# Spectrum channels grouped by parity, the second half's first inverse stage on 64-row tiles, and a new instruction order behind the first MLP

## The chip, the cores and the metric

The kernel runs on one core of a Trainium2 chip. The core has five instruction streams: TensorE (PE, matmuls, with its weight loads listed apart as PEld), ScalarE (ACT), VectorE (DVE), GpSimd (POOL) and SyncE (SP, which here only issues DMAs). The on-chip memory SBUF has 128 partitions; PSUM, where matmuls write, has 8 banks of 512 fp32 per partition. The metric is device microseconds of one execution, the median over several runs.

## The reference

The input `x` is 2048 tokens by 512 channels, bf16. Two kinds of layer alternate twice, each on a layer-normed copy and with a residual:

```python
x = A_q
x = x + _A_ref(_layernorm(x), A_k, A_v, A_shift_k, A_ssm_k, A_ssm_D)
x = x + _B_ref(_layernorm(x), B_w1, B_b1, B_w2, B_b2)
x = x + _A_ref(_layernorm(x), ...)      # the same weights again
x = x + _B_ref(_layernorm(x), ...)
...
# _A_ref: a 4-tap shift of k times v, a causal convolution over all 2048 tokens by FFT, times q
kv = k_shift * v
y = irfft(rfft(kv_pad) * rfft(ssm_k_pad))[:2048]
return q * (y + kv * ssm_D)
# _B_ref: gelu(layernorm(x) @ w1 + b1) @ w2 + b2, 512 -> 1376 -> 512
```

The convolution's `y` depends on `k`, `v` and the filters alone, so it is computed once and used by both A layers.

## The kernel before

**The convolution.** The tokens are cut into two halves of 1024, and the FFT into two stages of small DFTs, all as matmuls. For the filter (tags `h1`, `h2`) and for `kv` (`x1`, `x2`) `stage1` (line 553) makes DFTs over 128 tokens for eight sub-sequences, `stage2` (line 565) combines the eight with the table S2. Channels go in 64 groups of 8. After `stage2` a partition stands for a triple: one of 8 frequencies, one of the 8 channels `d` of a group, and real or imaginary part (the lowest bit). DVE multiplies the two spectra (line 464, 2048 elements wide), and for the second half adds a second product (tag `sum`). The inverse goes in two stages again: `inverse1` (line 665) with the table U, `inverse2` (line 683) with the table T2. `inverse1` is called once per half (tags `i1_0` and `i1_1`). One call makes 8 PSUM tiles of two banks; a tile is 8 groups of channels times two terms (cosine and sine side), that is 16 matmuls whose weights are the spectrum, 128 by 128 and read in steps of 4 elements (8 bytes), and whose moving operand is 128 columns of U. Each tile is evicted by one instruction of 1024 elements (line 469 on ACT, line 470 on DVE). In U a column of channel `d` has nonzero entries only in rows of the same `d`.

**Small filters.** The 4-tap shift is done on PE too. `shift` (line 610, first half) sends 11 shifted copies to each of two 64-row tiles of the array; per row tile the 11 moving operands have 2048 columns together, so 22 matmuls and 4096 columns a call. `shift_pair` (line 638, second half, tags `fir4` to `fir7`, two calls) uses four 32-row tiles: 88 matmuls and 8192 columns a call. Its keys come by eight transposing DMAs (line 766, tag `kt`), its values by plain loads on the same queue, and DVE multiplies its result with the values (line 647). `stage1` uses two column tiles (128 rows by 64 columns), all other matmuls the whole array.

**The MLPs.** Tokens go in 13 blocks: first half (1, 1, 2, 2, 2) row tiles of 128 tokens in layer pair one and (2, 2, 2, 2) in pair two, second half (4, 4) and (4, 4). For block b the tags are `q`b (statistics and norm), `y`b (times y, residual), `z`b (second norm), then `m1` (line 886: 11 tiles of 4 matmuls, N = 128 times the block's row tiles, Gelu on ACT, line 891) and `m2` (lines 920 and 909: 11 matmuls of 512 columns per row tile, issued in pieces of 4, 4 and 3, then an add on DVE, line 924). The normed rows are transposed by DMA (line 866), the first two by PE (line 874). The first-half blocks use nothing from `i1_1`; they fill PE while the second half's convolution is made. Block 9 is the first to read the second half's `y`, which comes from `inverse2` tagged `i2_1`.

**The order.** Every operation is numbered in program order. A constant list `SEQ` gives the order in which the 1185 operations go to their engines' in-order queues; a string `ENGS` chooses ACT, DVE or POOL where there is a choice; a string `BANKS` gives each PSUM tile its first bank. Waits follow from these: an operation waits for what it reads, and for the eviction of the tile that had its banks before. Numbers that matter below: `fir5` 296 and `fir7` 303 (the two `shift_pair` matmul groups), `x1_1` 308 to 322 (even: PE, odd: eviction), `x2_1` 324 to 355 with the sums 327, 331, ... 355, `i1_1` 356 to 371 (even: PE, odd: eviction, all eight on ACT), `i2_1` 372 to 381.

In the order of before, PE's eight `i1_1` tiles stand in two runs, one tile and then seven, with one piece of `m2` between. Their banks (each tile takes two) are 6, 4, 6, 2, 4, 6, 2, 4. Blocks that use split arrays behind the first MLP, each between whole-array work: [fir5], [one `x1_1` tile, then fir7], [one `x1_1`], [three], [three].

Of the kernel before, what the change touches and what calls it, by code (L numbers as in the profile page):

```python
# [36 lines left out]
class Prog:  # L37
# [60 lines left out]
    ENGS = ("apvpvvvpavaavaaaaaavvvaaavvvpvpvaavaaaaavaavvaaaaaaaavavaaaaaavaaavaaaaaappppaaaaaaaaaaaaaaaaaaaaaaaaaaaaapvvp"  # L98
            "paappvppaappvvvpaappaappaappaappaappaappvavpaappvappaappvvppvvvpaappvvavvvvvvavpvvvvppavavpvvvvvpvaaavpvvaaapv"
            "avva")  # L100
    BANKS = ("02220326464004602026041320002442462264542202240064064646402046462667062260046446220462640604660406064226644472"
             "44450442172316353547502206314500451400554567076567013226140174645320543403764701436154766316307007062272260403"
# [243 lines left out]
def _tables():  # L346
# [10 lines left out]
    S2 = np.zeros((2, 8, 8, 128, 2, 8, 8))  # L357
# [603 lines left out]
```

## Time and profile before

| | |
|---|---|
| median of 3 runs | 239.22 us (239.12 to 239.52) |
| span of the profiled execution, first to last instruction | 238.6 us |
| PE busy | 226.9 us |
| PE weight loads busy (beside PE) | 152.3 us |
| DVE busy | 178.1 us |
| ACT busy | 159.6 us |
| POOL busy | 55.3 us |
| matmuls of `inverse1`, both halves | 15.0 us, 256 |

The profile comes from one execution; what the runs show beyond its span (239.22 - 238.6 = 0.6 us) lies before the first and behind the last instruction. Its views used here: the page (shares, and the span in 40 slices whose digits are tenths of busy time), the chain of work that ended last (start, length and line of each piece), the groups by line and shape (xcount, then busy us and mean ns of one), timelines of one engine, and windows (busy time of each engine in a stretch). Matmul durations are latencies of pipelined instructions, so a rate is read from the length of a piece of the chain divided by its count. A few matmul records are missing, so a piece's count can be one short (x87 for 88).

### The profile page before, as it was taken

How to read it: one execution, taken by the hardware profiler on the slowest of the kernel's cores; microseconds unless marked ns; L12 is line 12 of the kernel's file. 1: busy time of each engine (PE TensorE's matmuls, PEld its weight loads, DVE VectorE, ACT ScalarE, POOL GpSimd, SP SyncE). 2: the span in 40 equal slices, each digit the busy share in tenths (PEclk: the TensorE clock that was granted, in tenths of full speed). 3: DMA queues.
4: the chain of work that ended last, by engine and by line, in shares of the span. 5: the costliest groups of instructions: out<-in, count | busy, mean ns of one | idle time of the engine just before them, and what ended most of it. 6: DMA issues, size and time to landing. Idle time of an engine off the chain costs nothing.

```text
span 238.6 us, 6251 instructions
## 1 busy us (share of the span) xinstructions
PE 226.9 (95%) x2615; PEld 152.3 (64%) x2637; DVE 178.1 (75%) x358; ACT 159.6 (67%) x255; POOL 55.3 (23%) x120
## 2 busy tenths in 40 slices
PE   6998698899999999999999999999999999999995
PEld 3897588885968588667769675644445444444454
DVE  0579869999999999999999999593579469404013
ACT  2586879999996899999768786359036606831630
POOL 2421030104623506446004522303020210200000
PEclk9999979999999999999999999999999999999999
DMA  6999767989946660053100304200300050132202
GB/s 173 350 393 388 272 181 186 257 267 194 163 87 197 153 140 3 1 69 103 54 0 15 80 0 83 49 3 12 78 0 3 18 157 0 25 66 91 84 0 91
DMA packets 41112, 26.75 MB, mean 112 GB/s; under 512 B 23702, under 2 KB 33788, under 8 KB 41084
## 3 DMA queue, kind: packets, MB, share of 16 engines
q1 hardware_dynamic: 40786, 26.20, 40.5%
q8 instruction: 21, 0.34, 0.6%
q10 hardware_dynamic: 298, 0.16, 0.3%
q14 instruction: 7, 0.06, 0.1%
HBM read 15.07 MB, written 2.10 MB: 72 GB/s over the span
## 4 chain that ended last, share of the span: by engine, by line
PE 83%; DVE 6%; DMA 4%; ACT 3%; issue 2%; POOL 1%; SPq 1%; POOLq 0%
PE ps L886 32%; PE ps L920 31%; PE ps L665 6%; PE ps L553 5%; PE ps L565 3%; ACT ar L469 3%; DMA ar<-in_A_ssm_k_dram 2%; DVE ar L464 2%; DMA ar<-ar 2%; DVE ar L616 1%; PE ps L683 1%; PE ps L909 1%; PE ps L638 1%; PE ps L610 1%; DVE ar L470 1%
## 5 line engine op out<-in xcount | busy, mean ns | idle before, releaser
L891 ACT ACTIVATE ar<-ps,sm 128x256 bf16<-128x256 f32 (+4 forms) x143 | 65.4, 525 | 41.0 <-PE ps L886 39.5
L469 ACT ACTIVATE ar<-ps 128x1024 bf16<-128x1024 f32 (+3 forms) x77 | 71.3, 1005 | 16.4 <-PE ps L553 6.4
L886 PE MATMUL ps<-ar 128*128 128x256 bf16 (+4 forms) x568 | 81.5, 297 | 0.3
L920 PE MATMUL ps<-ar 128*128 128x512 bf16 (+1 forms) x324 | 77.2, 379 | 1.1 <-issue 0.3
L886 PEld LDWEIGHTS ps<-ar 128*128 128x128 bf16 (+1 forms) x572 | 52.8, 100 | 28.1 <-ACT ar L891 0.4
L464 DVE TENSOR_TENSOR ar<-ar 128x512 bf16<-128x512 bf16 (+3 forms) x105 | 62.7, 637 | 0.9 <-ACT ar L469 0.4
L920 PEld LDWEIGHTS ps<-ar 128*128 128x128 bf16 (+1 forms) x341 | 32.4, 98 | 33.4 <-ACT ar L891 0.2
L924 DVE TENSOR_TENSOR ar<-ar,ps 128x512 bf16<-128x512 bf16 x31 | 20.7, 678 | 33.2 <-PE ps L920 33.0
L797 DVE BATCH_NORM_STATS2 sm<-ar 128x6 f32<-128x512 bf16 x64 | 42.9, 683 | 0.5
L822 ACT ACTIVATE ar<-ar,sm 128x512 bf16<-128x512 bf16 x34 | 26.4, 811 | 9.5 <-DVE sm L809 8.3
L804 POOL TENSOR_TENSOR sm<-sm 128x2 f32<-128x2 f32 (+2 forms) x26 | 23.6, 909 | 23.8 <-DVE sm L802 22.0
L802 POOL TENSOR_SCALAR sm<-sm 128x2 f32<-128x2 f32 (+2 forms) x21 | 6.4, 304 | 97.3 <-DVE sm L798 97.1
L553 PE MATMUL ps<-ar 128*64 128x128 bf16 x512 | 18.6, 227 | 3.1 <-issue 1.4
L565 PEld LDWEIGHTS ps<-ar 128*128 128x128 bf16 x512 | 18.4, 102 | 3.4 <-ACT ar L469 1.0
L565 PE MATMUL ps<-ar 128*128 128x64 bf16 x512 | 19.6, 199 | 0.5 <-ACT ar L469 0.4
L553 PEld LDWEIGHTS ps<-ar 128*64 128x64 bf16 x512 | 15.7, 114 | 6.1 <-issue 2.6
L812 POOL TENSOR_SCALAR sm<-sm 128x1 f32<-128x1 f32 x43 | 16.1, 390 | 2.0
L470 DVE CAST ar<-ps 128x1024 bf16<-128x1024 f32 x11 | 13.3, 1222 | 4.3 <-PE ps L565 2.8
L665 PE MATMUL ps<-ar 128*128 128x128 bf16 x256 | 15.0, 219 | 0.5 <-DVE ar L464 0.4
L665 PEld LDWEIGHTS ps<-ar 128*128 128x128 bf16 x256 | 14.7, 113 | 1.2 <-DVE ar L464 0.6
L823 DVE TENSOR_SCALAR ar<-ar,sm 128x512 bf16<-128x512 bf16 x30 | 11.8, 410 | 3.4 <-POOL sm L812 3.1
L470 DVE COPY ar<-ps 128x1024 bf16<-128x1024 bf16 (+1 forms) x9 | 5.5, 632 | 8.0 <-PE ps L516 5.3
(41 smaller groups left out, 94.3 us busy)
## 6 DMA issues: line engine op xcount, KB each, us to landing
ar<-tab_s SPq DMA_DIRECT2D x16, 256.0 KB, 9.0
ar<-ar SPq DMA_DIRECT2D x16, 256.0 KB, 3.7
ar<-in_A_ssm_k_dram SPq DMA_DIRECT2D x8, 256.0 KB, 6.8
ar<-in_A_q_dram SPq DMA_DIRECT2D x8, 256.0 KB, 4.7
ar<-in_A_v_dram SPq DMA_DIRECT2D x8, 256.0 KB, 6.1
out_dram<-ar SPq DMA_DIRECT2D x7, 256.0 KB, 2.5
ar<-in_B_w_dram SPq DMA_DIRECT2D x4, 344.0 KB, 4.8
ar<-in_B_w_dram SPq DMA_DIRECT2D x5, 256.0 KB, 4.0
```

What stands on the lines that cost most here:

```text
L464: return P.op(eng, lambda e: e.tensor_tensor(o, a, b, op), dur, reads=[a, b] + list(more), writes=[o])
L469: return e.activation(dst, src(), AF.Copy)
L470: return e.tensor_copy(dst, src())
L553: r = e.matmul(Q(tl, 64 * ri, 64, i * 128, [1, 128]), w, m, start=True, stop=True)
L565: r = e.matmul(Q(tl, 0, 128, i // 8 * 512 + i % 8 * 4, [32, 16], [1, 4]), w, m, start=True, stop=True)
L665: r = e.matmul(Q(tl, 0, 128, i * 128, [1, 128]), w, m, start=n == 0, stop=n == 1)
L797: P.op(DVE, lambda e, sj=sj, x=x: e.bn_stats(sj, x), 600.0, reads=[x], writes=[sj])
L804: P.op(POOL, lambda e: e.tensor_tensor(r, v, hf, ALU.pow), 420.0 + 149.0 * n, reads=[v, hf], writes=[r])
L822: return e.activation(o, x, AF.Identity, bias=u, scale=r)
L886: r = e.matmul(Q(tl, 0, rows, 0, [1, w]), a, m, start=dk == 0, stop=dk == 3)
L891: P.op(ACT, lambda e, dst=dst, tl=tl, rows=rows, bias=bias, w=w: e.activation(dst, Q(tl, 0, rows, 0, [1, w]), AF.Gelu_apprx_tanh, bias=bia ...
L920: r = e.matmul(Q(tl, 0, 128, 0, [1, 512]), ins[fc][0], ins[fc][1], start=fc == 0, stop=fc == 10)
```

## The change

Three things change.

1. **Tables.** In S2's output order and U's row order the partition index becomes (channel d, frequency, real/imaginary) in place of (frequency, d, real/imaginary), with the channels of a group in the order 0, 2, 4, 6, 1, 3, 5, 7. So all even channels of a group stand on partitions 0 to 63 and all odd ones on 64 to 127. The tables keep their sizes; real and imaginary part remain neighbours, as the swapping DMAs of the spectrum need.
2. **`inverse1` for the second half** (`split=True`). Each 128-row matmul with 128 columns becomes two 64-row ones with 64 columns: rows 0 to 63 with the columns of even channels, rows 64 to 127 with those of odd channels. The columns are picked from U in steps of 2 elements, and the two results go to the tile's two banks. A tile has 32 matmuls. Its eviction reads PSUM in runs of 32 and writes SBUF in steps of 2 elements (4 bytes).
3. **The order.** `SEQ` is as before in its first 330 places, up to the first MLP, and different behind; `ENGS` and `BANKS` differ in the same part. In the new order PE's `i1_1` tiles stand in two runs of four, the banks being 2, 4, 6, 2 and 4, 2, 6, 4: `368, 366, 364, 360`, then the last pieces of `m2` for two row tiles (682, 686), then `370, 358, 356, 362`, then three pieces of `m2` (735, 736, 737), then `i2_1` with 380. ACT evicts them in the order 369, 367, 361, 365, 371, 359, 357, 363. Split-array blocks behind the first MLP: [fir5], [one `x1_1` tile, then fir7], [four `x1_1`], [three], [four `i1_1`], [four `i1_1`]. `fir5` stands earlier among the MLP's matmuls, and the eight `kt` transposes stand earlier on SP's queue. The first MLP's `m1` tiles (N = 128) stand 19 in a row on PE, 17 before. The last `m2` piece of one row tile (686) stands ahead of `i1_1` before and between its two runs after, and two `y7` operations of DVE move from ahead of the last sum to behind it.

```diff
     SEQ = (
...
-        404, 450, 406, 489, 422, 451, 295, 532, 405, 423, 466, 407, 586, 460, 408, 454, 414, 467, 456, 294, 490, 491, 446,
...
-        345, 629, 660, 349, 661, 658, 754, 342, 355, 384, 327, 751, 382, 335, 719, 350, 346, 752, 755, 351, 347, 343, 331,
-        753, 721, 756, 715, 757, 758, 720, 759, 716, 727, 725, 632, 728, 383, 677, 664, 633, 665, 674, 801, 760, 726, 662,
-        733, 799, 672, 856, 659, 761, 663, 675, 668, 669, 666, 729, 680, 670, 860, 673, 762, 734, 763, 671, 667, 684, 678,
-        766, 800, 723, 802, 764, 730, 717, 731, 857, 858, 679, 685, 724, 862, 803, 718, 861, 859, 713, 714, 681, 686, 366,
-        722, 682, 732, 368, 863, 804, 367, 805, 864, 865, 866, 364, 806, 369, 360, 767, 809, 365, 810, 361, 358, 359, 765,
-        356, 357, 362, 370, 807, 811, 735, 808, 363, 812, 371, 683, 867, 813, 736, 374, 372, 737, 373, 873, 376, 868, 738,
...
+        451, 295, 282, 290, 289, 286, 207, 291, 283, 292, 285, 287, 586, 405, 416, 294, 293, 423, 448, 417, 456, 412,
...
+        727, 718, 680, 730, 355, 751, 713, 723, 675, 351, 667, 715, 714, 719, 728, 347, 725, 724, 721, 720, 733, 726,
+        343, 684, 734, 716, 731, 331, 685, 732, 722, 755, 681, 633, 752, 368, 753, 366, 369, 756, 860, 364, 367, 799,
+        360, 757, 682, 361, 801, 686, 365, 800, 759, 370, 758, 760, 358, 683, 371, 761, 762, 356, 802, 858, 359, 362,
+        803, 856, 763, 735, 357, 766, 804, 861, 857, 767, 859, 736, 764, 363, 862, 805, 737, 806, 765, 809, 863, 807,
+        380, 864, 810, 865, 811, 376, 381, 808, 814, 372, 377, 866, 739, 812, 876, 813, 873, 740, 874, 870, 815, 877,
...
-    S2 = S2.transpose(0, 1, 2, 3, 5, 6, 4).reshape(128, 128 * 128)
+    S2 = S2[..., [0, 2, 4, 6, 1, 3, 5, 7]].transpose(0, 1, 2, 3, 6, 5, 4).reshape(128, 128 * 128)
...
-    U = U.transpose(1, 2, 0, 3, 4, 5, 6).reshape(128, 256)
+    U = U[:, :, [0, 2, 4, 6, 1, 3, 5, 7]].transpose(2, 1, 0, 3, 4, 5, 6).reshape(128, 256)
...
-    def inverse1(p, q, Z):
+    def inverse1(p, q, Z, split):
...
                 for n, r in enumerate((p, q)):
-                    ins.append((i, n, A(0, 128, r + (dg // 4) * 512 + dg % 4, [4, 128]), A(0, 128, R_U + n * 128, [1, 128])))
+                    o = r + (dg // 4) * 512 + dg % 4
+                    if split:
+                        for g in range(2):
+                            ins.append((512 * g + 4 * i, n, A(64 * g, 64, o, [4, 128]), A(64 * g, 64, R_U + n * 128 + g, [8, 16], [2, 4])))
+                    else:
+                        ins.append((i * 128, n, A(0, 128, o, [4, 128]), A(0, 128, R_U + n * 128, [1, 128])))
...
-                    r = e.matmul(Q(tl, 0, 128, i * 128, [1, 128]), w, m, start=n == 0, stop=n == 1)
+                    r = e.matmul(Q(tl, 0, 128, i, *([32, 16], [1, 4]) if split else ([1, 128],)), w, m, start=n == 0, stop=n == 1)
                 return r
-            P.op(PE, f, 16 * 56.0, reads=[x for y in ins for x in y[2:]], tile=tl)
+            P.op(PE, f, 32 * 18.0 if split else 16 * 56.0, reads=[x for y in ins for x in y[2:]], tile=tl)
+            if split:
+                evac(BOTH, A(0, 128, Z + 64 * j, [1, 2], [512, 16], [2, 32]),
+                     lambda tl=tl: Q(tl, 0, 128, 0, [512, 2], [32, 16], [1, 32]), E1, tl)
+                continue
             evac(BOTH, A(0, 128, Z + 64 * j, [512, 16], [8, 8], [1, 8]),
                  lambda tl=tl: Q(tl, 0, 128, 0, [8, 16], [128, 8], [1, 8]), E1, tl)
...
-    inverse1(R_1, R_2, R_3)
+    inverse1(R_1, R_2, R_3, False)
...
-    inverse1(HH, HI, R_Z1)
+    inverse1(HH, HI, R_Z1, True)
```

More of the change, by code (lines that the diff above doesn't have):

```diff
@@ L44 @@
     SEQ = (
[53 rows of a table removed]
[L98 to L102, printed above, removed]
-             "71655156407602371631706316706615043246755274432051240747516203416017010")
[55 rows of a table added]
+    ENGS = (
+            "apvpvvvpavaavaaaaaavvvaaavvvpvpvaavaaaaavaavvaaaaaaaavavaaaaaavaaavaaaaaappppaaaaaaaaaaaaaaaaaaaaaaaaaaa"
+            "aapvvppaappvppaappvvvpaappaappaappaappaappvappavppaappaappaappvvppvappvapvvavapvavavvvvvvavpvvvapvvvvvpp"
+            "aaavpvavaappaaav")
+    BANKS = (
+            "02220326464004602026041320002442462264542202240064064646402046462667062220646062064026422060602220662246"
+            "42467462450041532313556442120552147601706751501205044354325435012213520542326730500110566052735231264334"
+            "36735543761643160751023162713162061264204041347162562550237740304676700461634470136")
     def __init__(self, nc):
```

95 rows, old and new, of the table SEQ are left out of this document.

## The prediction

> **What bounds the kernel now.** I read the page first: the shares, the slices, and the chain of work that ended last.
>
> ```profile
> span 238.6 us, 6251 instructions
> ...
> PE 226.9 (95%) x2615; PEld 152.3 (64%) x2637; DVE 178.1 (75%) x358; ACT 159.6 (67%) x255; POOL 55.3 (23%) x120
> ...
> PE   6998698899999999999999999999999999999995
> ...
> DVE  0579869999999999999999999593579469404013
> ...
> PE 83%; DVE 6%; DMA 4%; ACT 3%; issue 2%; POOL 1%; SPq 1%; POOLq 0%
> ```
>
> PE is the bound. DVE is nearly as full up to slice 27 (about 160 us), so it is the engine that could take over. Then the stages, by windows (length, then PE, weight loads, DVE, ACT, POOL busy, and the granted clock, which is full): from the first MLP matmul at 60.4 to the second half's inverse, the inverse's first stage, and two stretches behind it up to the last matmul.
>
> ```profile
> 60.40:124.70 64.30, 63.56 (x901) 48.02 (x912) 63.70 (x112) 56.23 (x112) 23.82 (x40) 1.00 0.41 89
> 124.70:132.80 8.10, 8.05 (x133) 7.55 (x132) 7.96 (x23) 6.40 (x7) 3.68 (x10) 1.00 0.16 34
> 132.80:156.90 24.10, 23.94 (x149) 14.88 (x152) 20.42 (x55) 14.61 (x28) 6.80 (x15) 1.00 0.21 46
> 156.90:236.20 79.30, 78.92 (x385) 37.71 (x391) 39.35 (x95) 36.07 (x59) 7.50 (x15) 1.00 0.16 44
> ```
>
> PE is idle for 0.74, 0.05, 0.16 and 0.38 us: 1.3 us in 175.8, and part of that is lost records. So behind 60.4 us a microsecond of PE work saved is one of time saved, unless a new wait takes it back, and a better order alone can bring at most those 1.3 us.
>
> **The matmuls of the split stage.** The chain of waits (start, length, piece):
>
> ```profile
> 15.83 1.89 PE ps L610 x44
> ...
> 72.12 1.05 PE ps L638 x87
> ...
> 84.55 3.06 PE ps L886 x28
> 87.61 0.57 PE ps L553 x16
> 88.18 2.73 PE ps L886 x24
> ...
> 105.01 0.47 PE ps L565 x16
> ...
> 124.95 0.90 PE ps L665 x16
> 125.84 0.65 PE ps L920 x3
> 126.49 6.26 PE ps L665 x112
> ...
> 188.42 9.68 PE ps L920 x44
> ```
>
> Removed: 128 matmuls of 128 columns at 6.26/112 = 55.9 ns, 16 to a tile: 0.895 us a tile, 7.16 us for eight. Added: 256 matmuls of 64 columns and 64 rows. One matmul of 64 columns in a row of sixteen takes 0.47/16 = 29.4 ns (line 565; it also writes PSUM in the new pattern, runs of 4 in steps of 32). If the two row groups run side by side, a pair takes 29.4 ns and a tile of 16 pairs 0.47 us; if not at all, 32 times 29.4 = 0.94 us. Those are the two ends. Line 610 is the nearest row, two row tiles of 64: 44 matmuls with 8192 columns. A column costs 9.68/44/512 = 0.43 ns on the whole array, so one after the other they would take 3.52 us; they took 1.89, with about 0.1 of that a change of array shape (below). The row groups do run side by side, nearly to the factor of two; with four row tiles line 638 moves 8192 columns in 1.05 us. The Trainium skill (TensorE: Matmul & The Clock Gate, Measured speedup vs the span model) gives a gain of only 3.07 for four row groups; by it a pair would take 29.4 x 4/3.07 = 38 ns. Line 638 has 3.52/1.05 = 3.4 or better, so the trace is kinder than the page.
>
> One thing differs from line 610: these weights are read in 8-byte steps.
>
> ```profile
> L886 PEld LDWEIGHTS ps<-ar 128*128 128x128 bf16 x520 | 47.4, 98 | 26.1 <-ACT ar L891 0.4 <-ACT ar L469 0.3
> ...
> L665 PEld LDWEIGHTS ps<-ar 128*128 128x128 bf16 x256 | 14.7, 113 | 1.2 <-DVE ar L464 0.6 <-issue 0.2
> ```
>
> Such a load takes 15 ns longer than a contiguous one. Behind 55.9 ns that is hidden; behind 29.4 it may show a little. I take 31 ns a pair, 0.50 us a tile, 4.00 us for eight: **3.16 us less PE work**, between 3.40 less and 0.36 more.
>
> **Changes of array shape.** The three rows from 84.55 show their price: line 886 takes 3.06/28 = 109 ns each, but 2.73/24 = 114 behind the split-array piece, so 0.11 us is lost on leaving; the piece itself has 0.57 for 16 matmuls of 128 columns, two side by side, 8 x 55.9 = 0.45, so 0.12 on entering. Behind the first MLP there were five split blocks with one change from one split shape to the other, 11 changes; after there are six such blocks, 13 changes. Two more at 0.1: **+0.2 us**.
>
> **Banks and evictions in the inverse.** ACT evicts all eight tiles (timelines of PE and ACT):
>
> ```profile
> 124.78 1.06 PE L665 MATMUL ps<-ar 128*128 128x128 bf16 x16
> ```
>
> ```profile
> 125.88 1.03 ACT L469 ACTIVATE ar<-ps 128x1024 bf16<-128x1024 f32 x1 [1.21 <-PE ps L665]
> 127.43 6.52 ACT L469 ACTIVATE ar<-ps 128x1024 bf16<-128x1024 f32 x7 [0.52 <-PE ps L665]
> ```
>
> An eviction starts 125.88 - 124.78 = 1.10 us after its tile's start, 0.20 after the PE work; the next follow every 6.52/7 = 0.93 us, and one lasts 1.03. So far PE's 0.90 a tile kept step with ACT's 0.93. Now PE is faster. Counted from the first tile: PE ends 368, 366, 364 at 1.50. Tile 360 takes the banks of 368, whose eviction runs from 0.70 to 1.73: **PE waits 0.23**. It ends at 2.23; a shape change and two m2 pieces (0.65 each, line 920) lead to 3.63, a change to 3.73. Tile 370 ends at 4.23, 358 at 4.73 (its banks were free at 3.59), 356 at 5.23 (free at 4.52). Tile 362 needs the banks of 370, whose eviction ends at 5.46: **PE waits another 0.23**, then ends at 5.96. Three m2 pieces of 2.37 us follow; the last eviction ends at 8.25, the first `i2_1` would start at 8.43: no wait. If m2 didn't stand there, 2.3 us of ACT's work would be bare. Sum **+0.5 us**; at 0.47 a tile it is 0.63, at 0.61 nothing, so this wait cushions an error in the tile's price.
>
> The eviction's write in 4-byte steps is not in the trace. All 67 ACT evictions of this size, whatever their pattern, average 1041 ns:
>
> ```profile
> L469 ACT ACTIVATE ar<-ps 128x1024 bf16<-128x1024 f32 x67 | 64.2, 1041 | 10.3 <-PE ps L553 6.4 <-PE ps L665 2.3 <-PE ps L565 1.4
> ```
>
> I take no change; the far end, twice the time, is a rival below.
>
> **The rest of the order.** What feeds the moved work?
>
> ```profile
> 60.40 3.97 PE L886 MATMUL ps<-ar 128*128 128x128 bf16 x68
> ```
>
> ```profile
> 60.84 5.54 ACT L891 ACTIVATE ar<-ps,sm 128x128 bf16<-128x128 f32 x20
> ```
>
> ```profile
> 60.77 5.78 SPq L766 DMA_TRANSPOSE ar<-in_A_k_dram  x4
> ```
>
> ```profile
> 122.85 1.21 DVE L464 TENSOR_TENSOR ar<-ar 128x2048 bf16<-128x2048 bf16 x1
> ```
>
> First MLP: a tile takes PE 3.97/17 = 0.23 us at most and ACT 5.54/20 = 0.28, so ACT falls 0.05 behind with each; 19 tiles in a row in place of 17 put about 0.1 to 0.3 on PE: **+0.2**. `fir5` moves ahead of three m2 pieces (4, 3 and 3 matmuls at 0.22) and one m1 tile (0.23), 2.4 us, from 72.12 to about 69.7. The eight `kt` transposes ended their issue at 66.55; on SP's queue they stand one behind the other now, behind one value load more, and end at about the same time, so the 5.6 us between issue and use become some 3, enough if they land as before. The last sum ends at 124.06, 0.72 before the first inverse tile: this is where DVE could take over. After, PE is there 0.65 (one m2 piece) and 0.2 (a split block, two changes, fewer ahead of it) earlier, DVE by 0.8 (two `y7` operations moved behind), so the 0.7 remains. DVE's norms of block 7 come later by two to four statistics, which the m2 pieces of block 6 ahead of block 7's m1 cover. I price these at nothing; each microsecond that DVE or SP is late beyond its cover is a microsecond of PE.
>
> **Sum.** -3.16 + 0.2 + 0.5 + 0.2 = -2.26 us: a span of 238.6 - 2.3 = 236.3, and with the 0.6 around it, which the median shows, **237.0 us**.
>
> **Rivals.** (1) *Half-way overlap*: a pair takes 38 ns. Then a tile takes 0.61, PE never waits for banks, and the change is -7.16 + 4.88 + 0.2 + 0.2 = -1.9: 237.3. For it: strided weights; against: line 610's factor. This is the page's number, read above. (2) *The new order has a wait* of a microsecond or more elsewhere, most likely DVE late for the sums or block 7, or the keys for `fir5`: 238.0 to 238.7. For it: DVE's row of nines, 0.7 us of cover at the sums and the 2.4 us taken from the keys; against: the order of before leaves PE idle for 1.3 us at most. (3) *The row groups run singly*, or the moving operand, picked in 4-byte steps that no row shows, streams at half speed: a pair takes 54 to 59 ns, a tile 0.87 to 0.94, the change is -0.2 to +0.36 plus 0.4: 239.4 to 240.0. Against: line 610. The Trainium skill (SBUF — State Buffer, Door 1) says that two reads in one 16-byte line suffice for full speed; the trace's 113 against 98 ns at exactly two disagrees for weights, and nothing here shows the moving side, which has four. (4) *Slower: the stepped eviction.* If ACT wrote 4-byte steps at half speed, eight evictions every 1.86 us would end at 0.7 + 7 x 1.86 + 2.0 = 15.7 in place of 8.3, and PE would stand 7.3 us before `i2_1`: 244. It decides from 1.3 us an eviction on, where the stall eats the 2.3 and 0.5 more. Against: 67 evictions that don't mind their pattern.
>
> **Chances and range.** Forecast 0.55 (its own range 236.4 to 237.6: a tile at 0.47 to 0.55, order waits of 0 to 0.6), (1) 0.15, (2) 0.15, (3) 0.09, (4) 0.06. The range 236.2 to 239.4 leaves out (4), most of (3) and a little below: about 0.15. This kernel's measurement can tell 0.2%, 0.5 us, from no change. Faster by that: 0.55 + 0.15 + 0.12 of (2) = 0.82. Within: 0.03 of (2) and 0.04 of (3), 0.07. Slower: 0.05 of (3) and 0.06 of (4), 0.11.
>
> **What would show it.** Right: in the chain, eight line 665 tiles of the second half at about 0.5 us for 32 matmuls, PE idle before the fourth and eighth, ended by ACT; ACT's evictions still 1.03 us; the same about 0.1 at each shape change. Wrong: tiles near 0.9; a DVE multiply (line 464) or a norm as the releaser of PE; evictions well over 1.1 us; PE idle for more than 2 us in all behind 60 us.

## The result and the profile after

The changed kernel takes 241.03 us (median of 20 runs, 238.63 to 242.75), the kernel of before in the same series 239.26 us (20 runs, 237.64 to 240.68). The ratio is 1.0065 with a 95% interval of 1.0046 to 1.0084: **slower by 0.65%, some 1.6 us**. It is taken over fast runs alone (one of the changed kernel's 20 was slow), so it is not the quotient of the two medians. The forecast was 237.0 us.

The page of the changed kernel (shares of the span, then the chain that ended last by engine):

```profile
span 238.2 us, 6507 instructions
...
PE 223.9 (94%) x2743; PEld 147.7 (62%) x2765; DVE 176.6 (74%) x353; ACT 163.5 (69%) x258; POOL 57.0 (24%) x122
...
PE 64%; ACT 15%; DVE 9%; POOL 5%; DMA 4%; issue 2%; SPq 1%; DVEq 0%; ACTq 0%
```

PE has 226.9 - 223.9 = 3.0 us less to do, so the split did what it says. But PE is no longer the chain: its share of the chain falls from 83% to 64%, and ACT's rises from 3% to 15%. The chain itself (start, length, piece) shows the two places, with line numbers of the changed kernel (473 is the eviction on ACT, 569 `stage2`, 674 `inverse1`, 696 `inverse2`, 825 and 835 belong to the norms):

```profile
105.16 3.19 POOL sm L825 x2
...
109.10 0.80 ACT ar L835
109.90 0.92 ACT ar L473
110.81 0.05 issue
110.86 0.64 PE ps L569 x16
...
124.17 0.67 PE ps L674 x32
124.85 0.02 issue
124.87 9.59 ACT ar L473 x8
134.45 0.04 issue
134.50 2.33 PE ps L696 x10
```

From 124.87 to 134.45 the end of the program is set by eight evictions on ACT, each 9.59/8 = 1.20 us, and not by matmuls at all. Earlier, at 110.86, an `x2_1` tile waits for an eviction that stands on ACT behind a norm, which waits for POOL. PE's timeline over the inverse (in brackets the idle time ahead of a group, and who ended it):

```profile
124.11 1.79 PE L674 MATMUL ps<-ar 64*128 64x64 bf16 x96
126.27 0.72 PE L674 MATMUL ps<-ar 64*128 64x64 bf16 x32 [0.37 <-ACT ar L473]
127.14 1.25 PE L933 MATMUL ps<-ar 128*128 128x512 bf16 x5 [0.16 <-issue]
128.33 1.25 PE L674 MATMUL ps<-ar 64*128 64x64 bf16 x64
129.81 0.72 PE L674 MATMUL ps<-ar 64*128 64x64 bf16 x32 [0.23 <-ACT ar L473]
131.00 0.72 PE L674 MATMUL ps<-ar 64*128 64x64 bf16 x32 [0.47 <-ACT ar L473]
131.88 2.32 PE L933 MATMUL ps<-ar 128*128 128x512 bf16 x10 [0.16 <-issue]
134.50 2.33 PE L696 MATMUL ps<-ar 128*128 128x512 bf16 x10 [0.29 <-ACT ar L473]
```

The groups are drawn with the latency of their last matmul, so waits are better read from start to start. The second and third tile start at 124.66 and 125.19: a tile takes 0.533 us, a pair of row groups 33.3 ns. By that the fourth tile could start at 125.72 and starts at 126.27; the waits are 0.55, 0.40, 0.66 and, ahead of `inverse2`, 134.50 - (131.88 + 10 x 0.2155) = 0.47 (0.2155 us is one `m2` matmul of 512 columns). Together 2.1 us.

**Where the time went, stage by stage.** A span also holds the stretch before the MLP, and there the first `m1` matmul starts anywhere from 57.9 to 60.4 us although every kernel here has the same order up to it. So I compare three stretches of PE's timeline: from the first MLP matmul to the first `i1_1` matmul, from there to the first `i2_1` matmul, and from there to the end of the last matmul. The last two columns are the runs: the ratio, and its excess over one as us of 239.

| kernel | to `i1_1` | to `i2_1` | to the end | sum | against before | ratio (95%) | us |
|---|---|---|---|---|---|---|---|
| before | 64.39 | 9.53 | 101.88 | 175.80 | | | |
| after | 65.04 | 10.39 | 101.33 | 176.76 | +0.96 | 1.0065 (1.0046 to 1.0084) | +1.6 |
| e1_runs | 66.19 | 8.78 | 101.31 | 176.28 | +0.48 | 1.0014 (0.9988 to 1.0039) | +0.3 |
| e2_order | 65.66 | 10.83 | 101.31 | 177.80 | +2.00 | 1.0119 (1.0087 to 1.0151) | +2.8 |
| e3_split | 64.48 | 10.64 | 101.88 | 177.00 | +1.20 | 1.0057 (1.0027 to 1.0087) | +1.4 |
| e4_split_runs | 64.48 | 8.75 | 101.88 | 175.11 | -0.69 | 0.9974 (0.9951 to 0.9996) | -0.6 |
| e9_again (= e4) | 64.48 | 8.74 | 101.88 | 175.10 | -0.70 | 0.9969 (0.9944 to 0.9994) | -0.7 |
| e6_tables | 64.39 | 9.53 | 101.88 | 175.80 | 0.00 | 1.0010 (0.9985 to 1.0035) | +0.2 |
| e7_norms | 65.44 | 8.79 | 101.31 | 175.54 | -0.26 | 1.0001 (0.9976 to 1.0025) | 0.0 |
| e5_two_dve | 64.49 | 14.84 | 101.87 | 181.20 | +5.40 | 1.0226 (1.0190 to 1.0263) | +5.4 |
| e8_dve_first | 64.48 | 8.09 | 104.48 | 177.05 | +1.25 | 1.0053 (1.0028 to 1.0079) | +1.3 |

One profile a kernel, but the sums go with the runs, to within 0.8 us throughout. (In the new order one `m2` piece of 0.65 us stands before `i2_1` that stood behind it, another inside the inverse that stood before it; so with no new waits its first stretch would be some 64.39 - 0.65 - 0.19 = 63.55, the 0.19 being the shape changes saved there.) Hence the balance of the change, in the trace: -2.89 for the tiles (8 x (0.895 - 0.533)), +0.2 for two more shape changes, +2.1 for waits on evictions in the inverse, +1.4 for what the order costs ahead of it (65.04 - 63.55, less the 0.09 of entering the first split tile, 64.48 - 64.39, which the shape changes hold): +0.8, where the table has +0.96.

Of the 1.4, 0.77 is the wait of the `x2_1` tile at 110.86 and 0.34 one ahead of `fir5`, both from start to start. The table also shows what the order gives back: the old order with the stepped eviction (e3) takes 10.64 us for the inverse, the new one 10.39 with two more `m2` pieces (1.29 us) in it.

### The profile page after: what moved, and what is told of

The parts are those of the page before. It is cut to its first block, busy times and chain, and to the rows that moved or that the text cites. A ratio compares the mean times of both kernels' runs of the same rounds, so it can differ in the third digit from the quotient of the medians.

```text
span 238.2 us, 6507 instructions
## 1 busy us (share of the span) xinstructions
PE 223.9 (94%) x2743; PEld 147.7 (62%) x2765; DVE 176.6 (74%) x353; ACT 163.5 (69%) x258; POOL 57.0 (24%) x122
## 4 chain that ended last, share of the span: by engine, by line
PE 64%; ACT 15%; DVE 9%; POOL 5%; DMA 4%; issue 2%; SPq 1%; DVEq 0%; ACTq 0%
PE ps L899 28%; PE ps L933 24%; ACT ar L473 13%; DVE ar L468 3%; PE ps L557 3%; POOL sm L825 3%; DMA ar<-in_A_ssm_k_dram 3%; PE ps L674 2%; DVE sm L810 2%; DMA ar<-ar 2%; ACT ar L835 2%; PE ps L696 2%; DVE ar L620 1%; PE ps L922 1%; PE ps L642 1%
## 5 line engine op out<-in xcount | busy, mean ns | idle before, releaser
L904 ACT ACTIVATE ar<-ps,sm 128x256 bf16<-128x256 f32 (+5 forms) x143 | 65.1, 525 | 36.3 <-PE ps L899 35.8
L473 ACT ACTIVATE ar<-ps 128x1024 bf16<-128x1024 f32 (+3 forms) x77 | 73.1, 1039 | 14.2 <-PE ps L557 5.9
L899 PE MATMUL ps<-ar 128*128 128x256 bf16 (+5 forms) x568 | 80.4, 297 | 0.3
L835 ACT ACTIVATE ar<-ar,sm 128x512 bf16<-128x512 bf16 x37 | 28.4, 811 | 12.7 <-DVE sm L822 7.5
L817 POOL TENSOR_TENSOR sm<-sm 128x2 f32<-128x2 f32 (+2 forms) x26 | 22.1, 851 | 18.5 <-DVE sm L815 16.6
L569 PE MATMUL ps<-ar 128*128 128x64 bf16 x512 | 18.3, 194 | 1.2 <-ACT ar L473 1.0
L569 PEld LDWEIGHTS ps<-ar 128*128 128x128 bf16 x512 | 16.9, 98 | 3.8 <-ACT ar L473 2.0
L825 POOL TENSOR_SCALAR sm<-sm 128x1 f32<-128x1 f32 x43 | 17.6, 424 | 2.0
L674 PE MATMUL ps<-ar 64*128 64x64 bf16 (+1 forms) x384 | 12.6, 203 | 1.5 <-ACT ar L473 1.1
L674 PEld LDWEIGHTS ps<-ar 64*128 64x128 bf16 (+1 forms) x384 | 11.9, 114 | 2.8 <-ACT ar L473 1.4
```

The lines of the kernel that those rows point to most:

```text
L473: return e.activation(dst, src(), AF.Copy)
L569: r = e.matmul(Q(tl, 0, 128, i // 8 * 512 + i % 8 * 4, [32, 16], [1, 4]), w, m, start=True, stop=True)
L674: r = e.matmul(Q(tl, 0, 128, i, *([32, 16], [1, 4]) if split else ([1, 128],)), w, m, start=n == 0, stop=n == 1)
L817: P.op(POOL, lambda e: e.tensor_tensor(r, v, hf, ALU.pow), 420.0 + 149.0 * n, reads=[v, hf], writes=[r])
L825: o = e.tensor_scalar(x, y, z, -1.0, ALU.mult, ALU.mult)
L835: return e.activation(o, x, AF.Identity, bias=u, scale=r)
```

## The experiments

Two parts of the change can be taken apart cleanly: the split with its eviction, and the order. Theory E of the expectations is that the eviction's stepped write makes ACT slow and so the loss; theory O is that the new order's other waits make it. The kernel of before took 238.73, 238.74 and 238.86 us in the series of these experiments, so they are compared by their ratios; a time that an expectation names is on the scale of the 239.26 above.

**e1: the same tile, evicted in unbroken runs.** The order of the loops in the eviction is turned, so that ACT reads one element from each of the two banks in turn and writes 64 neighbouring elements; everything else is the changed kernel.

```diff
-                evac(BOTH, A(0, 128, Z + 64 * j, [1, 2], [512, 16], [2, 32]),
-                     lambda tl=tl: Q(tl, 0, 128, 0, [512, 2], [32, 16], [1, 32]), E1, tl)
+                evac(BOTH, A(0, 128, Z + 64 * j, [512, 16], [2, 32], [1, 2]),
+                     lambda tl=tl: Q(tl, 0, 128, 0, [32, 16], [1, 32], [512, 2]), E1, tl)
```

> The changed kernel, but the second half's inverse evicts by reading the tile's two banks alternately and writing unbroken runs of 64 elements, in place of reading runs of 32 and writing every second element. Theory E (stepped writes make the eviction slow): ACT's evictions of this stage fall from a spacing of 1.17 us (8 in 9.57) to the 0.93 of the kernel before, PE's waits for them from about 2.0 us to 0.5, and the time by about 1.5 us, to 239.3 to 239.8. Theory O (the new order's other waits make the loss, the evictions are covered anyway): no more than 0.5 us faster than the changed kernel, 240.5 or more. If reading across banks is itself slow, the spacing stays at 1.1 us or above and this run decides nothing.

Measured 238.96 us (12 runs), ratio 1.0014 (0.9988 to 1.0039), which is 239.6 on that scale, as theory E had it. The evictions of the inverse in the changed kernel, by line within a window (least, median and greatest ns), two of the ten being `i2_1`'s:

```profile
L473 ACT ACTIVATE ar<-ps x10: 1017/1360/1399, 124.9 to 136.5; 128x1024 bf16<-128x1024 f32 x10
```

and in e1, the same view, and ACT's timeline:

```profile
L473 ACT ACTIVATE ar<-ps x10: 1018/1023/1045, 125.5 to 135.5; 128x1024 bf16<-128x1024 f32 x10
```

```profile
125.46 7.67 ACT L473 ACTIVATE ar<-ps 128x1024 bf16<-128x1024 f32 x8 [1.54 <-PE ps L674]
```

One eviction goes from 1.36 back to 1.02 us, eight from 9.57 to 7.67. It is the write and not the read: the `x2_1` evictions of the changed kernel read PSUM in exactly the pattern of the stepped one (two banks, 16 steps of 32, runs of 32), write runs of 32, and last 1.05 us at most (the same view, from 60 to 124 us, with all evictions of `x1_1` and `x2_1`):

```profile
L473 ACT ACTIVATE ar<-ps x16: 1001/1024/1049, 79.9 to 111.6; 128x1024 bf16<-128x1024 f32 x16
```

With the runs, the waits inside the inverse are 0.22 and 0.22 from start to start, as the prediction had reckoned for a pace of 0.93.

**e2: the order alone.** The changed kernel's `SEQ`, `ENGS` and `BANKS`, with the old matmuls and eviction.

```diff
-    inverse1(HH, HI, R_Z1, True)
+    inverse1(HH, HI, R_Z1, False)
```

> The changed kernel's order, choices of engine and banks, and its tables, but the second half's inverse on the whole array as before (16 matmuls of 128 columns a tile, evictions in runs of 8). What is left against the kernel before is the order alone. Both theories: PE does 8 x (0.895 - 0.533) = 2.9 us more than in the changed kernel. Theory E: 2.0 us of waits for slow evictions go, so about 0.9 slower than the changed kernel at the most, 241 to 242; against the kernel before the order alone then costs 1.5 to 2.5 us. Theory O: the waits that go are few, 2.5 to 3 us slower than the changed kernel, 243.5 to 244.

Measured 241.54 us (6 runs), ratio 1.0119 (1.0087 to 1.0151): 242.1 on that scale, just above theory E's 242 and well below theory O's 243.5. The new order without the split loses more than the whole change does, in the stretch ahead of the inverse (65.66 against 63.55) and in the inverse, where it only has more work. One of its waits can be seen in the chain of e1 (the same order), where block 2's first matmul of the MLP waits for the transposing DMAs of its norm:

```profile
65.15 1.52 ACT ar L835 x2
66.67 0.51 ACT ar L904 x2
67.17 0.50 ACT ar L835
67.67 4.37 DMA ar<-ar
72.04 0.05 issue
72.09 4.76 PE ps L899 x44
```

This wait is 0.9 us in e1, e2 and e7, and the one profile of the changed kernel, in the same order, has none. In those three the second of block 2's two transposes takes 4.3 to 4.4 us from issue to landing, in the changed kernel and the kernel of before 2.4 to 2.5; what makes it late isn't shown.

**e3 and e4: the order of before, with the split.** `SEQ`, `ENGS` and `BANKS` are those of before, tables and tiles those of the change; e3 evicts in steps, e4 in runs (the diff of e1).

> The kernel before with its own order, choices of engine and banks, but with the tables by parity and the second half's inverse split, stepped evictions included. Theory E: PE's tiles take 0.53 us, but eight evictions 1.17 apart end about 1 us later than the 0.93 ones did, and the next stage waits for them: 239.5 to 240.5, no gain. Theory O: the split gains what PE saves, 2 us or more: 236.5 to 237.5.

> As the run before (old order, split inverse), with the eviction that reads the banks alternately and writes unbroken runs. Theory E: evictions 0.93 apart, the last ends about 8.3 us after the stage's start where it was 9.2 in the kernel before, and the next stage starts earlier by about that: 238.0 to 238.8, faster than the kernel before. Theory O: like the run before, within 0.3 us of it.

e3 measured 240.41 us (11 runs), ratio 1.0057; e4 238.04 us (12 runs), ratio 0.9974, **faster than both kernels**; the same program once more (e9, below) gave 0.9969. Between e3 and e4 only the eviction's loops differ, and they are worth 10.64 - 8.75 = 1.9 us. On the scale of the expectations they are 240.6 and 238.6, near the upper ends of what theory E had; theory O had 237.5 at the most for e3 and is out. But e4 gains 0.7 where its PE work fell by 2.9. Its PE and ACT over the inverse:

```profile
122.38 0.72 PE L670 MATMUL ps<-ar 64*128 64x64 bf16 x32
123.03 0.82 PE L929 MATMUL ps<-ar 128*128 128x512 bf16 x3
123.78 2.57 PE L670 MATMUL ps<-ar 64*128 64x64 bf16 x128
126.54 0.72 PE L670 MATMUL ps<-ar 64*128 64x64 bf16 x32 [0.19 <-ACT ar L469]
127.46 0.72 PE L670 MATMUL ps<-ar 64*128 64x64 bf16 x32 [0.20 <-ACT ar L469]
128.38 0.72 PE L670 MATMUL ps<-ar 64*128 64x64 bf16 x32 [0.20 <-ACT ar L469]
129.52 1.67 PE L929 MATMUL ps<-ar 128*128 128x512 bf16 x7 [0.42 <-ACT ar L469]
131.13 1.04 PE L692 MATMUL ps<-ar 128*128 128x512 bf16 x4
```

```profile
124.55 6.52 ACT L469 ACTIVATE ar<-ps 128x1024 bf16<-128x1024 f32 x7 [0.39 <-PE ps L670]
```

The last tiles start 0.92 us apart (126.54, 127.46, 128.38) though each has 0.53 of work: that is ACT's pace, 6.52/7 = 0.93. The last eviction ends at 131.07, and `i2_1` starts at 131.13. From start to start the last four tiles wait 0.22, 0.38, 0.38 and 0.38, and the `m2` piece behind them about 0.5, together 1.9. The stage is now ACT's.

**e5: two of the eight evictions on DVE.** e4 with the third and the sixth eviction (365, 357) moved from ACT to DVE, by their letters in `ENGS` (written here as operation and engine).

```diff
-365 ACT, 357 ACT
+365 DVE, 357 DVE
```

> The kernel of e4_split_runs with the evictions 365 and 357 (third and sixth tile of the inverse's first stage) on DVE in place of ACT. Theory A, that what is left of the expected gain in e4 is lost to ACT's pace of 0.93 us an eviction: e4's waits of PE on ACT in this stage (0.19 + 0.20 + 0.20 + 0.42 = 1.0 us) shrink to under 0.3, and the time falls by 0.5 to 1.0 against e4: 237.0 to 237.5, ratio 0.993 to 0.995. Rival D, that DVE has no room there (its row of slices is full up to 155 us): the two evictions, 1.2 us each, delay its norms, and PE waits for those in place of ACT: 238.0 or more, ratio 0.997 and up.

Measured 244.19 us (6 runs), ratio 1.0226: far above theory A, and not in the way of rival D: what PE waits for is not a norm but an eviction itself, by its place in DVE's queue. DVE's timeline and PE's:

```profile
131.01 0.74 DVE L832 TENSOR_SCALAR ar<-ar,sm 128x512 bf16<-128x512 bf16 x2
131.66 1.22 DVE L470 CAST ar<-ps 128x1024 bf16<-128x1024 f32 x1
```

```profile
132.94 2.75 PE L670 MATMUL ps<-ar 64*128 64x64 bf16 x96 [4.81 <-DVE ar L470]
136.02 3.14 PE L929 MATMUL ps<-ar 128*128 128x512 bf16 x7 [0.33 <-issue]
139.00 1.03 PE L692 MATMUL ps<-ar 128*128 128x512 bf16 x4
```

The tile of 365 was done before 128 us; DVE came to it at 131.66, for statistics and norms of blocks 8 and 9 stand ahead of it on its queue. They had been work with time to spare; the eviction made them PE's critical path.

**e8 and e9: the same two evictions ahead of that work.** e8 is e5 with DVE's queue rearranged around them (the other queues unchanged); e9 is e4 again, beside it. The stretch of DVE's queue that moves:

```diff
-801, 760, 799, 856, 860, 766, 800, 802, 764, 857, 858, 862, 861, 859, 863, 806, 809, 365, 810, 357, 807, 811, 808, 812, 683
+801, 760, 365, 799, 766, 764, 357, 856, 860, 800, 802, 857, 858, 862, 861, 859, 863, 806, 809, 810, 683, 807, 811, 808, 812
```

> The kernel of e5_two_dve with DVE's queue rearranged: the evictions 365 and 357 stand ahead of most statistics and norms of blocks 8 and 9 (DVE order 801, 760, 365, 799, 766, 764, 357, 856, 860, ...), where their tiles are done; PE's and ACT's queues are those of e5. Theory A (ACT's pace is what is left, and e5 failed by the place on DVE alone): PE's waits in this stage fall from e4's 1.0 us to under 0.3, nothing stands at half clock, and the time is 237.0 to 237.6, 0.4 to 1.0 under e4. Rival D (DVE has no room for 2.4 us more): PE waits later for norms of blocks 8 or 9, and the time is that of e4 or above it (238.0 and up).

> The kernel of e4_split_runs once more (order of before, split, eviction in unbroken runs), as the measure beside e8 on the same chip and to narrow e4's interval: ratio 0.996 to 0.999 if the first figure was not chance; 1.000 or above if it was.

e8 measured 240.09 us, ratio 1.0053; e9 238.18 us, ratio 0.9969 (12 runs each). The inverse does get shorter, 8.09 against 8.74, but the next stretch longer, 104.48 against 101.88. PE's timeline of e8 behind the inverse:

```profile
135.42 0.61 PE L896 MATMUL ps<-ar 128*128 128x256 bf16 x4 [0.70 <-DVE ar L934]
...
138.04 1.10 PE L896 MATMUL ps<-ar 128*128 128x256 bf16 x8 [1.15 <-ACT ar L470]
```

Rival D holds for this arrangement: DVE has no room for the 2.4 us where they stand now; no other arrangement was run. The first wait is for DVE's add behind `m2`, the second ends with ACT, and in the chain it leads back over DVE's statistics, POOL and a norm. A third, at 139.32, is for ACT just behind that. From start to start the three are 0.87, 1.31 and 0.40, which is all of the lost 2.6 us.

**e6: the tables alone.** The order, matmuls and eviction of before, with the channels by parity.

> The order of before with the new channel tables alone: no split tiles, the old matmuls and evictions. Theory: the tables cost nothing, ratio 0.998 to 1.002 (238.3 to 239.2), and the 0.9974 of e4 is the split's. Rival: the channel order itself helps or hurts a stage (other partitions, other data), and the ratio lies outside those bounds; then e4's gain is not the split's alone.

Measured 238.91 us (12 runs), ratio 1.0010 (0.9985 to 1.0035); every stretch is that of before to 0.01 us. The tables cost nothing, and e4's gain is the split's.

**e7: two norms back on DVE.** e1 with the operations 654 and 709 (norms of blocks 5 and 6) on DVE, as in the order of before (again written as operation and engine).

```diff
-654 ACT, 709 ACT
+654 DVE, 709 DVE
```

> The kernel of e1_runs (new order, split, eviction in unbroken runs) with the two norms 654 and 709 back on DVE, where the order of before has them. Theory O, that the wait of 0.77 us of the tile 340 of x2_1 comes from its banks' eviction standing on ACT behind these norms: the wait falls under 0.2, and the time by 0.5 to 0.8: 238.2 to 238.5, ratio 0.998 to 0.999. Rival D, that DVE is as full as ACT there: PE's wait moves to the sums or to a norm of DVE, and the time stays within 0.3 of e1 (238.7 to 239.2, ratio 1.000 to 1.003).

Measured 238.49 us (12 runs), ratio 1.0001, 0.0013 below e1, which is inside both intervals: the runs can't tell the two apart. The trace shows half of what theory O asked for. The wait of the `x2_1` tile,

```profile
110.86 0.64 PE L569 MATMUL ps<-ar 128*128 128x64 bf16 x16 [0.61 <-ACT ar L473]
```

in the changed kernel, becomes in e7

```profile
112.27 0.64 PE L568 MATMUL ps<-ar 128*128 128x64 bf16 x16 [0.31 <-ACT ar L472]
```

that is, it falls by 0.3 us, as the runs do. The stretch ahead of the inverse falls by 0.75, to 65.44, but the other 0.48 is a wait ahead of `fir5` at 68 us that e1 has and e7 hasn't, long before either norm. The stretch is still 1.9 above the 63.55; the wait for block 2's transposes (0.89 in e7) is the largest of the rest. So the place of the norms is a small part of the order's cost and not all of it.

## Why the prediction was wrong, step by step

- **The matmuls: right, a little off.** A pair takes 33.3 ns where I took 31: -2.89 us in place of -3.16. The side-by-side rows held, and rival 1 (38 ns) and rival 3 (54 to 59) are out. The estimate from the figure of the Trainium skill (TensorE: Matmul & The Clock Gate, Measured speedup vs the span model) was 38; the trace again is kinder.
- **Shape changes: right.** About 0.1 each, two more.
- **The eviction: the first step that failed.** I took no change for its write in 4-byte steps, "67 evictions that don't mind their pattern". But every one of those 67 writes runs of 8 elements or more; no row had the new write. It lasts 1.36 us in place of 1.02 and follows every 1.20 in place of 0.93, some 1.9 us for the stage (e3 to e4). So rival 4 had the mechanism, and its threshold was wrong: "from 1.3 us an eviction on" looked only at the end of the stage. The tiles wait for their banks inside the stage too, and at 1.20 those waits are 0.55, 0.40 and 0.66. The term I had worked out for a pace of 0.93, two waits of 0.23, came out in e1 as 0.22 and 0.22: the working was right, and fed with the stepped evictions it gives about 2 us of waits in place of 0.5. That alone would have left a forecast of some -0.7, so it isn't the whole miss. The Trainium skill (SBUF — State Buffer, Door 1) has two hits in a 16-byte line enough for full speed; these writes have four in a line and take a third longer (1.36 us against 1.02), so the measurement decides against it for ACT's writes.
- **The order: the second step that failed, a term mis-sized.** I gave it 0.2; ahead of the inverse it costs 1.4 in the changed kernel, 2.5 in e1 and 2.1 in e2. Rival 2 had the kind, but its two places were wrong: DVE was not late for the sums, and `fir5`'s wait is 0.5 at most (0.34, 0.48 and none in after, e1 and e2). What I priced at nothing were two norms moved from DVE to ACT, where evictions of `x2_1` queue behind them (0.77 of wait; e7 takes 0.3 of it back), and the landing of block 2's transposes, which comes late in e1, e2 and e7. The rest of the order's cost is not taken apart. My argument "the order of before leaves PE idle for 1.3 us at most" bounds a gain and says nothing of a loss.
- **Either step was enough.** By the runs, the eviction put right alone leaves +0.3 (e1), the order put back alone +1.4 (e3), and only both together give a gain, 0.6 to 0.7 (e4, e9). The two losses do not simply add: with the stepped eviction the new order costs 1.6 - 1.4 = 0.2 us, no more than the noise, for its extra `m2` work in the inverse covers part of ACT's time; with unbroken runs it costs 0.3 + 0.6 = 0.9.
- **The baseline.** I set 0.6 us around the span. Where a run lists both, its time exceeds its span by 1.9 (the profiled execution of after: 240.1 and 238.2). So the profiled execution of before, with its MLP starting at 60.40, the latest of all here, was itself about 1.2 us above the median. The forecast isn't moved by it: it is the median less 2.26 either way.

Added up from the trace, +0.8 for -2.26: 1.6 by the waits on evictions (2.1 for 0.5), 1.2 by the order (1.4 for 0.2), 0.3 by the tiles. The runs show more loss than this, 1.6 us where the table has 0.96, and one profile can't place the rest: the profiled execution, at 240.1, was 0.9 faster than the median, and it lacks the wait of 0.9 for block 2's transposes that e1, e2 and e7 have. That other executions of the changed kernel have that wait isn't shown.

## What to carry to other kernels

When a matmul's output is laid out anew, look at the step in which the eviction writes as well as at the matmuls, and choose the order of its loops so that the writes are unbroken; reading two PSUM banks in turn cost nothing here. Before pricing a saving on PE, reckon the pace of the engine that empties its banks: at 0.93 us an eviction against 0.53 a tile, 2.9 us of saved work were worth 0.7. Moving an eviction to another engine moves it behind that engine's queue, and a queue that is nearly full turns spare work into PE's wait.

## What the runs showed of the hardware

ACT's evictions of 128 by 1024 elements slow from 1.02 to 1.36 us when bf16 is written in 4-byte steps, while reading alternately from two banks, element by element, leaves 1.02.

In e5, PE's standstill had a second price. Windows around it (window, its length, then PE, weight loads, DVE, ACT and POOL busy, granted clock):

```profile
131.00:132.00 1.00, 0.00 (x0) 0.00 (x0) 1.00 (x4) 0.00 (x0) 0.74 (x2) 1.00 0.08 13
132.00:133.00 1.00, 0.06 (x4) 0.07 (x6) 1.00 (x2) 0.00 (x0) 0.90 (x2) 0.58 0.59 118
133.00:134.00 1.00, 1.00 (x40) 1.00 (x42) 0.21 (x1) 0.00 (x0) 0.96 (x4) 0.50 0.62 190
...
138.00:139.00 1.00, 1.00 (x4) 0.31 (x3) 0.00 (x0) 0.00 (x0) 0.00 (x0) 0.51 0.09 16
139.00:140.00 1.00, 1.00 (x6) 0.49 (x5) 0.00 (x0) 0.00 (x0) 0.00 (x0) 1.00 0.00 0
```

After 4.8 us without a matmul the granted clock is 0.50 and stays there until 139, for 6 us of work (6.8 us at half rate in all): tiles start 0.85 us apart in place of 0.53, and seven `m2` matmuls take 139.00 - 136.02 = 2.98 us in place of 1.5. The Trainium skill (TensorE: Matmul & The Clock Gate, Part 1: The HAM clock gate (the "warmup" mystery)) names half rate after an idle window of about 3.4 us and full rate after about as much sustained work; the halving agrees, and the return took longer here, the 6 us above. In the other kernels no wait of PE between 120 and 145 us is longer than 1.4 us, and their clock is 1.00 there.
